# A gated attention and FFN kernel: two-tile attention steps, a later place for attention in the scheduler's order, weight splits finished by an accumulating DMA, and x operands kept in DRAM

## The chip, the cores and the metric

The kernel runs on one core of a Trainium2 chip. The metric is the device time of one execution in microseconds (us). Three executions of the kernel before are known; their median is 679.92 us.

## The reference, cut to what matters

```python
x = A_x                                            # 1 x 2048 x 512, float32
g = sigmoid((x * gate_w).sum(-1, keepdims=True))
qkv = x @ wqkv                                     # 512 x 1536; 32 heads of 16 channels
# query s looks at keys s, s-2, ..., s-14 (8 of them, dilation 2); masked where negative
a = softmax(q . k / 4) @ v  ->  2048 x 512  @ wo   # 512 x 512
b = (gelu_tanh(x @ w_gate) * (x @ w_up)) @ w_down  # 512 x 1792, 512 x 1792, 1792 x 512
out = g * a + (1 - g) * b
```

Everything is float32. The kernel splits each matmul operand into a high part, rounded to the matmul's float32r type, and a low part, the remainder, and multiplies high by high, high by low and low by high: three matmuls for each product.

## The kernel before, in words

**Parity halves.** Dilation 2 means that even and odd tokens never meet in attention. All work is done per parity (`par` 0 and 1), 1024 tokens each: 8 tiles of 128 tokens (`NP`), or 2 blocks of 512 (`blk`).

**Stages, in the order of the text.** (1) Six projections, `project(par, cb)`: `cb` 0 and 2 give q and k of one half of the heads, `cb` 1 gives v and the gate. Their results go to DRAM (`KS`, `QS`, `VS`). (2) `ffn(0)`: 14 steps `f` of `gate_up`, each with 7 products of 6 matmuls (a Strassen-like scheme over two weight matrices, gate and up: operands of x named a11, a12, a22, s1 to s4, operands of the weights named b11, b21, b22, t1 to t4), and from step 2 on four `down` pieces of 6 matmuls that belong to the pair of steps before. (3) `finish(0)`: 96 matmuls that add attention times `wo` onto the down result. (4) `ffn(1)` and `finish(1)`, the same for the odd tokens.

**Attention as filler.** `attention()` is a Python generator over 8 units (parity, 128 channels). For each unit it loads k, q and v in shifted slots, and does `scores` (per tile a product of 8 x 128 values and a reduction), `softmax`, and `mix` (per tile a product, three halving additions, and per four tiles a transpose whose result goes to DRAM, `OS`). All of that arithmetic is VectorE's. `pull(budget)` advances the generator after each projection tile, each group of products and each `down`; every `yield` gives the microseconds that a piece is reckoned at. So attention's instructions lie between FFN's. The framework's scheduler then simulates the program and takes ready instructions by their place in that order; every engine and every DMA queue executes its own list in order.

**Weights of a step.** `fetch(f)` loads gate and up weights (SP's DMA queue), `combine(f)` forms t1 to t4 with three VectorE subtractions, and `operands(par, f)` splits the seven operands one by one: ScalarE copies to the high part (line 68), GpSimd subtracts to the low part (line 69), and SP stores the pair to DRAM (`WS`, line 362). Parity 1 loads those pairs back (line 359) and neither combines nor splits again. `down_w` does the same for the down weights (`DS`, lines 368 and 374).

**VectorE's part of an FFN step.** `add` (line 390) reads a PSUM bank and thereby frees it, `hidden` multiplies (line 394) and, for parity 0, subtracts for the low part (line 397; for parity 1 GpSimd does that). There are four rotating PSUM banks (`p`) and four that accumulate (`acc0` to `acc3`).

**x operands.** `operands_0` forms s1 to s4 of parity 0 during the projections. `operands_1` forms all operands of parity 1 during the last FFN step and `finish(0)`: four loads, eight VectorE sums (lines 114 to 117), 14 ScalarE copies and 14 GpSimd subtractions.

Of the kernel before, what the change touches and what calls it, by code (L numbers as in the profile page):

```python
# [16 lines left out]
P = 128  # L17
# [12 lines left out]
WARM = 31  # L30
BT = 4
MASKED = -1e9 * DH ** 0.5

OPS = ("b11", "t1", "t2", "b21", "b22", "t3", "t4")
# [3 lines left out]
def tile_gated_mix(ctx: ExitStack, tc: tile.TileContext, xt, wqkv, wff, wo, out):  # L38
# [6 lines left out]
    BUFS = {"A": 16, "S": 16, "w": 14, "d": 4, "raw": 2, "t": 1, "hh": 6, "hl": 6, "c": 4, "s": 3,  # L45
            "r": 2, "rt": 4, "p": 4, "lg": 2}
    COLS = {"w": 2 * WQ, "c": 2 * WQ, "d": 1024, "t": 1024, "raw": WT}

    def tl(tag, dt=F32):
        return pool.tile([P, COLS.get(tag, 512)], dt, name=tag, bufs=BUFS[tag])  # L50

# [20 lines left out]
    KS, VS, QS, OS, WS, DS = {}, {}, {}, {}, {}, {}  # L72
    for par in range(2):
        for hh in range(2):
            for n, t in (("k", KS), ("v", VS)):
                t[par, hh] = dram.tile([2, W + S // 2, UC], F32, name=f"{n}s{par}{hh}")
                for c in range(2):
                    nc.gpsimd.dma_start(t[par, hh][c, :W], zero)
            QS[par, hh] = dram.tile([2, S // 2, UC], F32, name=f"qs{par}{hh}")
        for u in range(NU):  # L80
            for half in range(2):
                OS[par, u, half] = dram.tile([32, 4, BT * P], F32, name=f"os{par}{u}{half}")


    early = iter(["c", "rt"] * 99)
    X, WC = {}, {}

    def load_xk(kc, blk, first=False):
        hi, lo = tl("A", F32R), tl("A", F32R)
        X[0, blk, kc] = hi, lo  # L90
        for a, n in ((0, P), (P, 512 - P)) if first else ((0, 512),):
            raw = tl(next(early))
# [4 lines left out]
    def load_cb(cb, kc, eng, tag=None):  # L97
        hi, lo = tl("w", F32R), tl("w", F32R)
        WC[cb, kc] = hi, lo
        raw = tl(tag or "c")  # L100
        if cb == 1:
            n = 2 * WQ
            for hh in range(2):
                nc.sync.dma_start(raw[:, hh * WQ:(hh + 1) * WQ], wqkv[hh, 2, :, kc * WQ:(kc + 1) * WQ])
        else:
            n = 512
            nc.sync.dma_start(raw[:, :n], wqkv[cb // 2, kc // 2, :, kc % 2 * 512:kc % 2 * 512 + 512])
        return lambda: split(eng, hi[:, :n], lo[:, :n], raw[:, :n])

    def sums(par, kc, a, b, eng, put, eng2=None):  # L110

        t = tl("t")
        s1, s2, s3, s4 = t[:, :512], t[:, 512:], b[:, :512], a[:, 512:1024]
        eng.tensor_tensor(s1, b[:, :512], b[:, 512:1024], op=OP.add)
        eng.tensor_tensor(s2, s1, a[:, :512], op=OP.subtract)
        eng.tensor_tensor(s3, a[:, :512], b[:, :512], op=OP.subtract)
        eng.tensor_tensor(s4, a[:, 512:1024], s2, op=OP.subtract)
        for n, s in (("s1", s1), ("s2", s2), ("s4", s4), ("s3", s3)):
            hi, lo = tl("S", F32R), tl("S", F32R)
            split(eng2 or eng, hi, lo, s)  # L120
            put(n, hi, lo)
            yield

    def raw_pair(par, kc):
        ab = []
        for blk in range(2):
            raw = tl("raw")
            nc.sync.dma_start(raw[:, :1024].rearrange("p (a c) -> p a c", a=2), xt[2 * par + blk, :, kc:kc + 3:2, :])
            ab.append(raw)
        return ab  # L130

    XOP, nxt = {}, {}

    def load_x1():
        for kc in range(2):
            a, b = raw_pair(1, kc)
            for blk, raw in ((0, a), (1, b)):
                for i in range(2):
                    if blk == 1 and (kc, i) != (1, 1):
                        d = tl("d", F32R)  # L140
                        hi, lo = d[:, :512], d[:, 512:]
                    else:
                        hi, lo = tl("hh", F32R), tl("hl", F32R)
                    X[1, blk, kc + 2 * i] = hi, lo
                    split(nc.vector, hi, lo, raw[:, i * 512:(i + 1) * 512])

    def operands_0():
        for kc in range(2):
            a, b = raw_pair(0, kc)
            for _ in sums(0, kc, a, b, nc.vector, lambda n, hi, lo: XOP.__setitem__((n, kc), (hi, lo))):  # L150
                pass
# [3 lines left out]
    def operands_1(first):  # L155
        for kc in range(2):
            a, b = raw_pair(1, kc) if kc else first
            for n, raw in (("a11", a[:, :512]), ("a12", a[:, 512:1024]), ("a22", b[:, 512:1024])):
                nxt[n, kc] = tl("A", F32R), tl("A", F32R)
                split(nc.gpsimd, *nxt[n, kc], raw)  # L160
                yield
            yield from sums(1, kc, a, b, nc.vector, lambda n, hi, lo: nxt.__setitem__((n, kc), (hi, lo)), nc.gpsimd)
# [69 lines left out]

    def scores(par, u):
        k, q = LG[par, u]
        lg = pool.tile([P, NP, W, UH], F32, name="lg", bufs=2)
        for jj in range(NP):
            prod = pool.tile([P, W, UC], F32, name="prod")
            nc.vector.tensor_tensor(prod, k[:, jj:jj + W, :], q[:, jj, None, :].to_broadcast([P, W, UC]), op=OP.mult)  # L238
            nc.vector.tensor_reduce(lg[:, jj].rearrange("p w h -> p (w h)"),  # L239
                                    prod.rearrange("p w (h d) -> p (w h) d", d=DH), axis=AX.X, op=OP.add)  # L240
            yield 2.5
# [21 lines left out]
    def mix(par, u):  # L263
# [4 lines left out]
        tb = pool.tile([P, NP, UC], F32, name="tb")  # L268
        for jj in range(NP):
            if jj % BT == 0:  # L270
                o = pool.tile([P, BT, UC], F32, name="o")
            prod = pool.tile([P, W, UC], F32, name="prod")
            nc.vector.tensor_tensor(prod.rearrange("p w (h d) -> p w h d", d=DH),  # L273
                                    v[:, jj:jj + W, :].rearrange("p w (h d) -> p w h d", d=DH),
                                    lg[:, jj, :, :, None].to_broadcast([P, W, UH, DH]), op=OP.mult)
            yield 1.2
            nc.vector.tensor_tensor(prod[:, :4], prod[:, :4], prod[:, 4:], op=OP.add)  # L277
            nc.vector.tensor_tensor(prod[:, :2], prod[:, :2], prod[:, 2:4], op=OP.add)  # L278
            nc.vector.tensor_tensor(o[:, jj % BT], prod[:, 0], prod[:, 1], op=OP.add)  # L279
            yield 1.4  # L280

            if jj % BT == BT - 1:
                nc.vector.transpose(tb[:, jj + 1 - BT:jj + 1].rearrange("p t c -> p (t c)"),
                                    o.rearrange("p t c -> p (t c)"))
                for a in range(4):
                    nc.sync.dma_start(OS[par, u, jj // BT][:, a], tb[32 * a:32 * a + 32, jj + 1 - BT:jj + 1])
# [29 lines left out]
    def pull(budget, key=None):  # L316
        credit[0] += budget
        while credit[0] > 0 and (key is None or key not in done):
            c = next(fill, None)
# [11 lines left out]
    RAW = {}  # L331

    def fetch(f):
        raw = tl("raw")
        nc.sync.dma_start(raw[:, :1024], wff[f, :, :1024])
        RAW[f] = [raw]

    def combine(f):

        raw, t = RAW[f][0], tl("t")  # L340
        quart = raw[:, :1024].rearrange("p (a b) -> p a b", a=4)
        b11, b21, b12, b22 = (raw[:, i * 256:(i + 1) * 256] for i in range(4))
        t1, t3, t2, t4 = (t[:, i * 256:(i + 1) * 256] for i in range(4))
        sub = lambda o, a, b: nc.vector.tensor_tensor(o, a, b, op=OP.subtract)  # L344
        sub(t[:, :512].rearrange("p (a b) -> p a b", a=2), quart[:, 2:], quart[:, 0::2])
        sub(t2, b22, t1)
        sub(t4, b21, t2)
        RAW[f] = dict(b11=b11, b21=b21, b22=b22, t1=t1, t2=t2, t3=t3, t4=t4)
# [307 lines left out]
```

## Time and profile before

| | us |
|---|---|
| three runs | 678.1, 679.92, 680.22 (median 679.92) |
| the profiled execution, its own time | 680.39 |
| its span in the profile | 678.6 |
| PE, DVE, ACT, POOL busy in the span | 631.2, 584.4, 313.8, 236.1 |
| mean granted TensorE clock | 0.967 |

PE is TensorE's matmuls, PEld its weight loads, DVE is VectorE, ACT ScalarE, POOL GpSimd, SPq the DMA queue that SyncE issues. "idle before" is the time in which an engine stood still just ahead of the instructions of a group, and the arrow names what ended most of it. L390 is line 390 of the kernel before. Three stages can be told by the PE's lines: projections from 4.2 to 144.0 us, `ffn(0)` with `finish(0)` to 435.4 us, `ffn(1)` with `finish(1)` to 674.5 us.

### The profile page before, as it was taken

Reading aid. Unit: us, or ns where it says so; the run is one execution under the profiler, and the core shown is the slowest. Engines: PE = TensorE matmul, PEld = TensorE weight load, DVE = VectorE, ACT = ScalarE, POOL = GpSimd, SP = SyncE. Lnnn points to the kernel's source line nnn. Section 1 sums busy time; section 2 is a strip of 40 time slices with the busy share of each in tenths; the row PEclk is TensorE's granted clock in tenths of the full one; section 3 lists DMA queues with packets and bytes.
Section 4 is the critical chain, followed back from the end, with each engine's and each line's share of the span. In section 5 each row is a group of like instructions: output and inputs, shape, how many; then the busy total and the mean of one; then the engine's idle time right before and its main releaser. Section 6 shows DMA issues by size and latency. Waiting matters only on the chain.

```text
span 678.6 us, 8894 instructions
## 1 busy us (share of the span) xinstructions
PE 631.2 (93%) x2839; PEld 512.9 (76%) x2839; DVE 584.4 (86%) x714; ACT 313.8 (46%) x601; POOL 236.1 (35%) x198
## 2 busy tenths in 40 slices
PE   8998999996799979997989849999999999999997
PEld 6888998874587758875868637888777888887785
DVE  5439899879999999989999988998999999989432
ACT  4424442245446455655454564234434644454562
POOL 5204014066737364634471760023122221224220
PEclk9999999998799989998998978999999999999999
DMA  8885755597966665675457587776566766544163
GB/s 254 269 253 172 247 156 187 172 300 250 310 235 218 243 229 171 234 252 208 156 191 224 159 225 158 249 234 218 179 187 197 214 196 197 185 124 127 36 104 124
DMA packets 116046, 136.46 MB, mean 201 GB/s; under 512 B 42400, under 2 KB 68640, under 8 KB 116000
## 3 DMA queue, kind: packets, MB, share of 16 engines
q1 hardware_dynamic: 115488, 135.84, 63.8%
q8 instruction: 22, 0.36, 0.2%
q14 instruction: 24, 0.20, 0.1%
q0 software_dynamic: 512, 0.07, 0.1%
HBM read 81.80 MB, written 54.07 MB: 200 GB/s over the span
## 4 chain that ended last, share of the span: by engine, by line
DVE 41%; PE 38%; DMA 7%; issue 6%; ACT 4%; SPq 1%; POOL 1%; DVEq 0%; POOLq 0%; ACTq 0%
PE p L381 21%; DVE prod L273 6%; PE p L420 6%; PE acc L420 5%; DVE prod L238 5%; DVE prod L277 4%; DVE lg L239 4%; DMA raw<-xt 4%; PE acc L557 3%; PE p L557 3%; DVE t L344 3%; DVE c L394 3%; DVE c L390 2%; DVE prod L278 2%; DVE o L279 2%
## 5 line engine op out<-in xcount | busy, mean ns | idle before, releaser
L381 PE MATMUL p<-S,w 128*128 128x512 f32 x672 | 176.6, 406 | 10.2 <-DVE c L390 4.1
L381 PEld LDWEIGHTS p<-S,w 128*128 128x128 f32 x672 | 130.8, 195 | 42.8 <-DVE c L390 4.5
L381 PE MATMUL p<-A,w 128*128 128x512 f32 x504 | 135.6, 407 | 16.2 <-DVE c L390 16.0
L381 PEld LDWEIGHTS p<-A,w 128*128 128x128 f32 x504 | 97.1, 194 | 42.4 <-DVE c L390 20.0
L397 POOL TENSOR_TENSOR hl<-c,hh 128x512 fp32r<-128x512 f32 x28 | 44.7, 1595 | 168.5 <-ACT hh L396 141.4
L238 DVE TENSOR_TENSOR prod<-k,q 128x1024 f32<-128x1024 f32 x64 | 86.8, 1356 | 11.5 <-DMA q<-qs 10.6
L273 DVE TENSOR_TENSOR prod<-v,lg 128x1024 f32<-128x1024 f32 x64 | 81.5, 1273 | 6.7 <-DMA v<-vs 5.3
L420 PE MATMUL p<-d,hh 128*128 128x512 f32 x224 | 71.7, 405 | 10.5 <-ACT p L414 10.4
L239 DVE TENSOR_REDUCE lg<-prod 128x64 f32<-128x1024 f32 x64 | 77.7, 1214 | 1.1
L69 POOL TENSOR_TENSOR w<-t,w 128x256 fp32r<-128x256 f32 x56 | 58.4, 1056 | 48.2 <-ACT w L68 38.5
L396 ACT ACTIVATE hh<-c 128x512 fp32r<-128x512 f32 x56 | 35.3, 631 | 80.3 <-DVE c L394 80.0
L69 POOL TENSOR_TENSOR w<-raw,w 128x256 fp32r<-128x256 f32 x42 | 43.0, 1034 | 63.8 <-ACT w L68 60.6
L277 DVE TENSOR_TENSOR prod<-prod 128x512 f32<-128x512 f32 x64 | 59.0, 922 | 1.3
L420 PEld LDWEIGHTS p<-d,hh 128*128 128x128 f32 x224 | 43.0, 194 | 22.0 <-ACT p L414 11.8
L420 PE MATMUL acc<-d,hh 128*128 128x512 f32 x224 | 57.7, 394 | 0.7 <-ACT hh L396 0.7
L420 PEld LDWEIGHTS acc<-d,hh 128*128 128x128 f32 x224 | 41.8, 188 | 11.7 <-ACT hh L396 2.4
L394 DVE TENSOR_TENSOR c<-c 128x512 f32<-128x512 f32 x56 | 44.6, 796 | 5.2 <-ACT c L482 4.8
L385 ACT ACTIVATE s<-p 128x512 f32<-128x512 f32 x56 | 32.8, 593 | 26.2 <-PE p L381 26.2
L390 DVE TENSOR_TENSOR c<-p,s 128x512 f32<-128x512 f32 x56 | 38.0, 681 | 8.0 <-PE p L381 7.8
L420 PE MATMUL p<-d,hl 128*128 128x512 f32 x112 | 42.9, 394 | 0.0
L429 ACT ACTIVATE rt<-p 128x512 f32<-128x512 f32 x48 | 28.6, 595 | 29.4 <-PE p L420 28.0
L177 PE MATMUL p<-w,A 128*128 128x512 f32 (+2 forms) x192 | 38.5, 345 | 2.9 <-ACT w L68 1.1
(125 smaller groups left out, 1002.0 us busy)
## 6 DMA issues: line engine op xcount, KB each, us to landing
ws<-w SPq DMA_DIRECT2D x98, 256.0 KB, 2.9
w<-ws SPq DMA_DIRECT2D x98, 256.0 KB, 2.7
raw<-wff SPq DMA_DIRECT2D x14, 512.0 KB, 5.0
ds<-d SPq DMA_DIRECT2D x14, 512.0 KB, 3.9
d<-ds SPq DMA_DIRECT2D x14, 512.0 KB, 4.5
raw<-xt SPq DMA_DIRECT2D x12, 512.0 KB, 5.4
k<-ks SPq DMA_DIRECT2D x8, 512.0 KB, 5.0
q<-qs SPq DMA_DIRECT2D x8, 512.0 KB, 6.3
```

Of the source, the lines that this page charges most:

```text
L69: eng.tensor_tensor(lo, raw, hi.bitcast(F32), op=OP.subtract)
L177: nc.tensor.matmul(ps[:, :cn], a[:, t], w[:, c0:c0 + cn], start=(kc == 0 and n == 0), stop=(kc == KC - 1 and n == 2))
L238: nc.vector.tensor_tensor(prod, k[:, jj:jj + W, :], q[:, jj, None, :].to_broadcast([P, W, UC]), op=OP.mult)
L239: nc.vector.tensor_reduce(lg[:, jj].rearrange("p w h -> p (w h)"), prod.rearrange("p w (h d) -> p (w h) d", d=DH), axis=AX.X, op=OP.add)
L273: nc.vector.tensor_tensor(prod.rearrange("p w (h d) -> p w h d", d=DH), v[:, jj:jj + W, :].rearrange("p w (h d) -> p w h d", d=DH), lg[:, ...
L277: nc.vector.tensor_tensor(prod[:, :4], prod[:, :4], prod[:, 4:], op=OP.add)
L381: nc.tensor.matmul(ps, w_, a_, start=(start and kc == 0 and n == 0), stop=(kc == 1 and n == 2), skip_group_check=True)
L390: nc.vector.tensor_tensor(c, ps, s, op=OP.add)
L394: nc.vector.tensor_tensor(ge, ge, up, op=OP.mult)
L397: eng.tensor_tensor(hl_, ge, hh_.bitcast(F32), op=OP.subtract)
L420: nc.tensor.matmul(pp, a[:, ts], w, start=(i == 0 and n == 0 and gr == 0), stop=(i == 1 and n == 2), skip_group_check=True)
L557: nc.tensor.matmul(pa, a, b, start=False, stop=(u == NU - 1 and n == 2), skip_group_check=True)
```

## The change

1. *Two tiles per attention instruction.* `scores` and `mix` handle two token tiles in each VectorE instruction (`spans` gives overlapping windows of k or v), so half as many instructions do twice the elements each. `OS` is laid out so that `channels` reads it back with one DMA of 2 KB rows instead of four with rows of 128 bytes.
2. *Order.* `pull` runs the generator under a priority 150 places later (`BEHIND`).
3. *Weight splits.* `operands(f)` works on two groups (three and four operands side by side): ScalarE writes minus the high part into the low part's place, a GpSimd-issued DMA with `accum_op=add` adds the raw weights onto it, and ScalarE writes the high part. GpSimd's subtractions and the stores to and loads from `WS` and `DS` are gone; for parity 1 weights are fetched, combined and split anew.
4. *Queues.* Weight fetches, the reloads of x operands, and the output stores of parity 0 are issued by GpSimd.
5. *x operands of parity 1* are formed in `load_x1` at the start, stored to DRAM (`keep`) and reloaded one by one (`operands_1(n)`) in the last step of `ffn(0)`.
6. Buffers are laid out anew for that; the first loads find 12 places instead of 8.

The core of the diff:

```diff
+BEHIND = 150
+GROUPS = (("t1", "t2", "b11"), ("b22", "t3", "t4", "b21"))
...
+    def keep(n, kc, hi, lo):
+        x = XS[n, kc] = dram.tile([P, 1024], F32, name=f"x{n}{kc}")
+        nc.gpsimd.dma_start(x[:, :512], hi.bitcast(F32))
+        nc.gpsimd.dma_start(x[:, 512:], lo.bitcast(F32))
...
     def load_x1():
...
+            for n, x in sums(a, b):
+                hi, lo = pair("S")
+                split(nc.vector, hi, lo, x)
+                keep(n, kc, hi, lo)
...
+    def operands_1(n):
+        for kc in range(2):
+            t = tl("A" if n[0] == "a" else "S", F32R)
+            nc.gpsimd.dma_start(t.bitcast(F32), XS[n, kc])
+            XOP[n, kc] = t[:, :512], t[:, 512:]
...
+    def spans(t, jj):
+        a = t[:, jj:jj + W, :]
+        return bass.AP(a.tensor, a.offset, [a.ap[0], [UC, 2], [UC, W], [1, UC]])
...
     def scores(par, u):
-        for jj in range(NP):
-            prod = pool.tile([P, W, UC], F32, name="prod")
-            nc.vector.tensor_tensor(prod, k[:, jj:jj + W, :], q[:, jj, None, :].to_broadcast([P, W, UC]), op=OP.mult)
...
-            yield 2.5
+        for jj in range(0, NP, 2):
+            prod = pool.tile([P, 2, W, UC], F32, name="prod")
+            nc.vector.tensor_tensor(prod, spans(k, jj), q[:, jj:jj + 2, None, :].to_broadcast([P, 2, W, UC]), op=OP.mult)
+            yield 2.3
...
+            yield 2.3
...
     def pull(budget, key=None):
...
-            c = next(fill, None)
+            with tc.high_priority(offset=-BEHIND):
+                c = next(fill, None)
...
     def fetch(f):
-        nc.sync.dma_start(raw[:, :1024], wff[f, :, :1024])
+        nc.gpsimd.dma_start(r[:, 2::5], q[:, :2])
+        nc.gpsimd.dma_start(r[:, 3:5], q[:, 2:])
...
-    def operands(par, f):
+    def operands(f):
+        for i, ops in enumerate(GROUPS):
+            n = len(ops) * QW
+            w = tl(f"g{i}", F32R)
+            hi, lo = w[:, :n], w[:, n:2 * n]
...
+            nc.scalar.activation(lo, raw, AF.Copy, scale=-1.0)
+            nc.gpsimd.dma_start(lo.bitcast(F32), raw, accum_op=OP.add)
             yield
+            nc.scalar.activation(hi, raw, AF.Copy)
+            yield
...
-    def down_w(par, f):
+    def down_w(f):
         d = WD[f] = tl("d", F32R)
...
+        split(nc.gpsimd, d[:, :512], d[:, 512:], RD.pop(f))
...
+        def anew(*names):
+            if not par and f == FC - 1:
+                for n in names:
+                    operands_1(n)
...
+    def ahead():
+        combine(0)
+        AGAIN[0] = operands(0)
...
     def channels(par, u, half):
-        for b in range(4):
-            nc.sync.dma_start(o[32 * b:32 * b + 32].rearrange("p (m j) -> p m j", j=32), src[b])
+        nc.sync.dma_start(o, OS[par, u, half].rearrange("b i a c -> (b i) (a c)"))
...
-                    nc.sync.dma_start(out_v[2 * jj + par, :, c], r[:, c])
+                    (nc.sync if par else nc.gpsimd).dma_start(out_v[2 * jj + par, :, c], r[:, c])
```

## The prediction

> **What bounds the kernel now.** I first read the page's busy times (PE 93%, DVE 86%), then cut the span at the PE's lines into projections, parity 0 (`ffn(0)`, `finish(0)`) and parity 1. Busy time per stage (matmuls counted in brackets), with granted clock at the end:
>
> ```profile
> 4.20:144.00 139.80, 136.85 (x771) 118.63 (x770) 106.52 (x138) 52.31 (x125) 28.84 (x29) 1.00 0.72 223
> 144.00:435.40 291.40, 253.55 (x1022) 200.32 (x1021) 276.65 (x330) 151.44 (x296) 150.34 (x127) 0.92 0.67 218
> 435.40:674.50 239.10, 237.60 (x1021) 190.73 (x1019) 199.70 (x244) 108.16 (x180) 53.91 (x35) 1.00 0.56 169
> ```
>
> The columns are length, PE, PEld, DVE, ACT, POOL, clock, DMA. The parities have the same matmuls, but parity 0 takes 291.4 us and parity 1 239.1: 52.3 us are lost in parity 0, where DVE is 95% busy and the clock is 0.92. A clock of 0.92 over 291 us is worth 23 us; the rest is standing still. Parity 1 shows that the PE can be kept busy at full clock beside a DVE at 84%. Next, the waits (total us, times, longest):
>
> ```profile
> PEld p L381 <- DVE c L390: 24.5, 10, 5.2
> ...
> PE p L381 <- DVE c L390: 20.1, 7, 4.8
> ...
> PE p L420 <- ACT p L414: 10.4, 2, 7.7
> ```
>
> The PE waits for DVE's `add`, which frees a PSUM bank. The timeline shows one such wait:
>
> ```profile
> 313.47 1.49 DVE L344 TENSOR_TENSOR t<-raw,t 128x256 f32<-128x256 f32 x1
> 314.89 1.34 DVE L279 TENSOR_TENSOR o<-prod 128x128 f32<-128x128 f32 x1
> 316.15 0.41 DVE L344 TENSOR_TENSOR t<-raw,t 128x256 f32<-128x256 f32 x1
> 316.49 1.21 DVE L273 TENSOR_TENSOR prod<-v,lg 128x1024 f32<-128x1024 f32 x1
> 317.62 1.27 DVE L390 TENSOR_TENSOR c<-p,s 128x512 f32<-128x512 f32 x2
> ```
>
> The PE starts again at 318.95, 4.79 us late. DVE was behind with work that the PE does not need, and two of those instructions took over a microsecond more than their like. The twin at 316.15 took 0.41, not 1.49, and POOL was subtracting beside the slow ones. Sizes without that disturbance come from the groups in 420 to 440 us, where POOL has no work, and with it from those in 140 to 400:
>
> ```profile
> L273 DVE TENSOR_TENSOR prod<-v,lg 128x1024 f32<-128x1024 f32 x5 | 6.1, 1213 | 0.1
> L277 DVE TENSOR_TENSOR prod<-prod 128x512 f32<-128x512 f32 x5 | 3.4, 688 | 0.1
> L278 DVE TENSOR_TENSOR prod<-prod 128x256 f32<-128x256 f32 x5 | 2.1, 421 | 0.1
> L279 DVE TENSOR_TENSOR o<-prod 128x128 f32<-128x128 f32 x5 | 1.4, 288 | 0.1
> ```
>
> ```profile
> L397 DVE TENSOR_TENSOR hl<-c,hh 128x512 fp32r<-128x512 f32 x27 | 26.4, 977 | 3.4 <-ACT hh L396 3.3
> ...
> L277 DVE TENSOR_TENSOR prod<-prod 128x512 f32<-128x512 f32 x24 | 24.1, 1004 | 0.4
> ```
>
> So a DVE instruction costs about 0.16 us plus 1.03 ns per element (0.688 less 0.421 for 256 elements more), and beside POOL 0.3 us more on average.
>
> **Part by part: DVE in parity 0 (276.7 us now).** *Disturbance:* over the groups of 140 to 400 us, busy time less count times clean mean is 4.4 (L238), 3.1 (L273), 7.6 (L277), 4.5 (L278), 4.2 (L279), 7.8 (L397), 6.2 (L394) and 8.1 (L344): 46 us, over POOL's 127 instructions there, or 0.36 us each. The change leaves some 21 of those (14 down splits, 4 of `wo`, 3 masks): 8 us. Minus 38. *Two tiles:* three units of attention are 144 instructions here, 72 fewer at 0.16: minus 11.5. *Sums of `operands_1`* (L114 to L117, 15.5 us for 16, of which the early eight are clean): minus 10. *More attention:* a unit is reckoned at 45.4 before and 41.4 after, so the same budgets pull a tenth more, about 0.3 unit of 43 us: plus 13. Sum 230 us.
>
> **DVE in parity 1 (199.7 now).** Minus 11.5 for two tiles, minus 13 for the attention done earlier, plus 14 `combine` of 0.688 + 2 x 0.421 = 1.53, or 21, plus 5 for 14 more POOL subtractions: 201 us.
>
> **From DVE's load to time.** Per 237.6 us of matmuls DVE had 1.16 in parity 0, which then took 291.4 us, and 0.84 in parity 1, which took 239.1: 161 us for each unit between. At 230 us (0.97) the straight line gives 260 us. But most of the 52 us is sheer excess over the PE's time, so below 1 the loss should fall faster than the line; with none, it is 239. I take 254, nearer the line, since attention's instructions are now up to 2.3 us long and an `add` can stand behind one. Parity 1 (0.85) gives 241, and I add 1 for ACT's longer list.
>
> [...]
>
> **The order.** Of two ready instructions FFN's goes first. That costs nothing if attention is ready for `finish(0)`: by the budgets (108 in projections, 125 up to the last `down`) some five units are pulled by then and four are needed, so a delay of 150 places, about one step of 16 us, hides in a spare unit of 43. Without that cover, `finish(0)` would wait out those 16 us.
>
> **Weight splits.** Per step, seven ScalarE copies of 0.411 become four of 768 or 1024 elements:
>
> ```profile
> L396 ACT ACTIVATE hh<-c 128x512 fp32r<-128x512 f32 x56 | 35.3, 631 | 80.3 <-DVE c L394 80.0
> ...
> L68 ACT ACTIVATE w<-t 128x256 fp32r<-128x256 f32 x56 | 22.2, 411 | 10.8 <-DVE t L344 9.5 <-POOL w L69 1.3
> ...
> L78 POOL DMA_DIRECT2D ks<-zero x8 | 4.3, 540 | 1.1 <-DVE zero L62 0.9 <-issue 0.2
> ```
>
> At 0.22 per 256 elements they take 0.85 and 1.07, 3.8 us a step: ACT gains 0.95 a step in parity 0 (151 to 165 us of 254) and 4.5 with the down weights in parity 1 (108 to 171 of 242, or 70%). That lies beside PE's work while the copies that PE waits for pass in time. POOL loses 95 us of weight subtractions in parity 0.
>
> The accumulating DMA is not in this trace. Below, it is a copy:
>
> ```profile
> ws<-w SPq DMA_DIRECT2D x98, 256.0 KB, 2.9
> ...
> ds<-d SPq DMA_DIRECT2D x14, 512.0 KB, 3.9
> ```
>
> Above, it also reads its target, so twice 3.9. I take 5 us for 384 or 512 KB. It is issued early in step f for step f+1; about 13 us of cover remain, so either end costs nothing; past the cover each us costs 28 over the 28 steps. DMA volume falls by 66 MB (`ws`, `w`, `ds`, `d`) and grows by 11 (second weight fetch), 15 (x operands) and the 26 that the accumulation writes. SP's queue, which stood 99.5 us for POOL at L362 ahead of attention's loads, is freed of all that.
>
> POOL now issues five DMAs a step: two `fetch`, two accumulations, one `fetch_d`. The only row is 0.54 us, for 8 partitions. If the cost does not grow with partitions it stays there; if it grows in proportion, 128 cost 8.6. SP's issues of 128-partition loads stand at 0.39 to 0.55 in the timeline, so I take 1.1, near the low end. Queued behind such a DMA on POOL are the down split, the mask, and in parity 1 the low parts of `hidden`, for which `down` waits a step later. On DVE, `combine` waits for such a fetch, with `add` and attention queued behind it. Today that costs 1.3 us in all (L344 <- raw, the groups' idle column), and the fetch is issued half a step ahead as before, so I count nothing; 1 us late in each step would cost up to 28.
>
> **x operands, start.** Eight more VectorE splits and 28 DMAs of 256 KB. None of it stands ahead of the first projections; DMA engines are at 0.86 in the first 40 us, and 4.2 MB at 250 GB/s may push the first k and q loads back by up to 17 us, where DVE is nearly idle (5.4 of 20 us between 20 and 40). PE's cost: 0, up to 5 if the loads for `cb` 1 are late. The reloads, 7.3 MB (some 36 us at 200 GB/s), are hidden by the last step and `finish(0)`; uncovered, they cost a few us at one place.
>
> **Sum.** 4.2 (head) + 140 + 254 + 242 + 4.1 (tail) = 644 of span, and 1.8 around it as now (680.39 less 678.6): 646. The profiled execution stands 0.5 above the median, which changes nothing. Ends: 239 for both parities gives 628; parity 0 on the straight line, parity 1 at 250 and 3 us more at the start give 663.
>
> **Rivals.** *ACT takes DVE's place.* PE's next product needs W's copy and the bank seeds (L414 already holds it for 10.4 us), and longer instructions stand in that list. For it: ACT at 70% in parity 1. Against: PE has other groups of 6 matmuls between. If each step loses 1 us, 28 steps give 674; the same comes out if the accumulation outlasts its cover by 1 us.
>
> *POOL becomes the bound, and the kernel is slower.* In parity 1 POOL has per step two subtractions of 1.6 (L397), a down split of 1.6 and five issues of x: 4.8 + 5x against 16 us. It decides from x = 2.3 on; x = 2.7 uses up nearly the whole gain, and x = 3 costs 14 x 3.8 = 53 us in parity 1 and some in parity 0, so about 700. For it: x is between 0.54 and 8.6. Against: SP's issues. [...]
>
> *The change does not do what it says.* If readiness and not place decides DVE's order, the `add` waits stay where both are ready: that is the straight line, 652, within the forecast's own range.
>
> **Chances.** Forecast 0.60 (628 to 663); ACT or the accumulation late 0.17 (664 to 677); no change 0.03; slower 0.20, mostly POOL. About 0.3% (2 us) is what a measurement of this kernel can tell from no change. Range 626 to 690: it leaves out the dearer half of the slow cases and a little below.
>
> **What would show it.** DVE under 235 us in parity 0, L390's `add` no longer PE's longest wait, clock near 1.00, parity 0 near 254 us and parity 1 near 242; DMA issues on POOL near 1 us. Wrong if POOL is over 90% busy in parity 1, if `hi`/`lo` tiles or their DMA end PE's waits, or if parity 0 stays over 275 us.

## The result and the profile after

The changed kernel takes 688.15 us (median of four runs, 684.21 to 689.42), the kernel before beside it 679.27: ratio 1.0122 [1.0076, 1.0168]. It is slower by 1.2%; the forecast was 646. Of all timed runs below one, of e6, was a slow one (696.56 us at the lowest clock of its four), and e6's median leaves it out. The profiled execution has a span of 687.2 us against 678.6. Cut at PE's lines as before, with PE's standstill between the parities left out (the windows view of the kernel after; columns are length, PE, PEld, DVE, ACT, POOL, clock, DMA share, GB/s):

```profile
4.20:150.20 146.00, 139.49 (x772) 120.32 (x771) 113.86 (x120) 58.21 (x129) 45.14 (x58) 0.99 0.86 264
150.20:415.40 265.20, 245.61 (x1021) 193.06 (x1019) 241.38 (x254) 156.78 (x248) 99.04 (x109) 0.98 0.64 173
424.50:683.40 258.90, 246.70 (x1020) 196.59 (x1020) 184.21 (x188) 150.77 (x241) 122.18 (x112) 0.96 0.49 122
```

So the difference of 8.6 us of span is made of plus 6.2 in the projections (139.8 before), minus 26.2 in parity 0 (291.4), plus 9.1 in a standstill that was not there, and plus 19.8 in parity 1 (239.1); the tail gives 0.3 back. Of the gain of 37 us forecast for parity 0, 26 came. It was spent in three places for which the sum had almost nothing. In parity 1 VectorE has 15 us less work than before, and the stage is 20 us longer. PE's column shows how: the same matmuls take 246.7 us there instead of 237.6, at a clock of 0.96 instead of 1.00, so 9.1 of the 19.8 us are slow matmuls behind pauses, and 10.7 are pauses.

Who waits for whom (the waits of the kernel after: total us, times, longest):

```profile
DVE raw L404 <- DMA raw<-wff: 24.8, 12, 5.4
...
PEld p L435 <- DVE c L444: 21.6, 11, 3.7
ACT d L76 <- DMA r<-wff: 21.1, 6, 7.9
...
PE p L435 <- DVE c L444: 17.0, 9, 3.2
...
DVE raw L151 <- DMA raw<-xt: 12.5, 2, 12.3
...
PE p L435 <- ACT s L662: 9.0, 1, 9.0
```

PE and PEld wait for the same banks, so each pause shows in both lines. The `add` (L444, L390 before) is still the largest item of PE's own waits, 17.0 us in 9 waits where it was 20.1 in 7. Three waits for transfers are new or have grown: `combine` for weights (1.3 us before), the down split (L76) for its weights (2.4 before), and `sums` (L151) for x. The last line is the standstill between the parities. Its timeline:

```profile
410.48 5.48 POOL L77 TENSOR_TENSOR d<-r,d 128x512 fp32r<-128x512 f32 x1 [1.44 <-ACT d L76]
...
416.26 0.55 POOL L398 DMA_DIRECT2D r<-wff  x1 [0.30 <-POOL d L77]
...
418.62 0.90 POOL L398 DMA_DIRECT2D r<-wff  x1
421.45 0.63 ACT L76 ACTIVATE d<-r 128x512 fp32r<-128x512 f32 x1 [7.86 <-DMA r<-wff]
...
423.88 1.06 ACT L662 ACTIVATE s<-p 128x512 f32<-128x512 f32 x2
...
424.51 2.07 PE L435 MATMUL p<-A,g 128*128 128x512 f32 x4 [8.96 <-ACT s L662]
```

A GpSimd subtraction took 5.48 us; one of the same shape at 277.49 us, with no VectorE instruction beside it, took 1.26. The down-weight fetch (L398) is behind it on GpSimd's list, ScalarE's copy of those weights waits 7.86 us for the fetch, and behind that copy on ScalarE's list stand the output copies (L662) that free PE's banks. The subtraction explains some 4 of the 9 us (5.48 less 1.26, an estimate). The rest is the fetch itself, which takes 5.2 us from its issue at 416.26 to the copy at 421.45 (the median of these fetches is 3.1), and two more copies of weights on ScalarE ahead of L662.

### The profile page after: what moved, and what is told of

The parts are those of the page before. It is cut to its first block, busy times and chain, and to the rows that moved or that the text cites. A ratio compares the mean times of both kernels' runs of the same rounds, so it can differ in the third digit from the quotient of the medians.

```text
span 687.2 us, 8278 instructions
## 1 busy us (share of the span) xinstructions
PE 635.1 (92%) x2839; PEld 513.2 (75%) x2839; DVE 546.4 (80%) x572; ACT 370.7 (54%) x623; POOL 275.5 (40%) x294
## 4 chain that ended last, share of the span: by engine, by line
PE 37%; DVE 21%; DMA 18%; issue 11%; ACT 6%; POOL 4%; SPq 2%; DVEq 0%; POOLq 0%; ACTq 0%
PE p L435 22%; PE acc L474 6%; PE p L474 6%; DMA raw<-wff 5%; DVE prod L325 4%; DVE raw L404 3%; DMA g<-raw 2%; DVE prod L329 2%; DMA raw<-xt 2%; DMA raw<-wqkv 2%; PE acc L651 2%; DMA v<-vs 2%; PE p L651 2%; DVE c L448 1%; DVE prod L331 1%
## 5 line engine op out<-in xcount | busy, mean ns | idle before, releaser
L435 PE MATMUL p<-S,g 128*128 128x512 f32 x672 | 176.3, 406 | 15.0 <-ACT p L510 5.8
L435 PEld LDWEIGHTS p<-S,g 128*128 128x128 f32 x672 | 129.8, 195 | 48.9 <-ACT p L510 7.9
L435 PE MATMUL p<-A,g 128*128 128x512 f32 x504 | 135.9, 409 | 20.8 <-DVE c L444 11.8
L435 PEld LDWEIGHTS p<-A,g 128*128 128x128 f32 x504 | 98.1, 197 | 47.6 <-DVE c L444 15.1
L421 POOL DMA_DIRECT2D g<-raw x56 | 50.3, 898 | 157.4 <-ACT g L420 141.7
L325 DVE TENSOR_TENSOR prod<-v,lg 128x2048 f32<-128x2048 f32 x32 | 74.2, 2318 | 6.1 <-DMA v<-vs 5.6
L404 DVE TENSOR_TENSOR raw<-raw 128x256 f32<-128x256 f32 (+1 forms) x84 | 56.7, 677 | 24.9 <-DMA raw<-wff 24.8
L289 DVE TENSOR_TENSOR prod<-k,q 128x2048 f32<-128x2048 f32 x32 | 74.4, 2324 | 1.2 <-DMA qs<-r 1.0
L291 DVE TENSOR_REDUCE lg<-prod 128x128 f32<-128x2048 f32 x32 | 72.9, 2279 | 0.1
L77 POOL TENSOR_TENSOR d<-r,d 128x512 fp32r<-128x512 f32 x28 | 51.3, 1838 | 33.3 <-ACT d L76 32.5
L420 ACT ACTIVATE g<-raw 128x1024 fp32r<-128x1024 f32 (+1 forms) x56 | 53.2, 950 | 13.1 <-DVE raw L404 10.5
L444 DVE TENSOR_TENSOR c<-p,s 128x512 f32<-128x512 f32 x56 | 37.6, 681 | 25.6 <-PE p L435 25.6
L423 ACT ACTIVATE g<-raw 128x1024 fp32r<-128x1024 f32 (+1 forms) x56 | 53.0, 946 | 0.0
L474 PEld LDWEIGHTS acc<-d,hh 128*128 128x128 f32 x224 | 41.9, 188 | 10.7 <-ACT hh L450 1.1
```

Of the source, the lines that this page charges most:

```text
L77: eng.tensor_tensor(lo, raw, hi.bitcast(F32), op=OP.subtract)
L289: nc.vector.tensor_tensor(prod, spans(k, jj), q[:, jj:jj + 2, None, :].to_broadcast([P, 2, W, UC]), op=OP.mult)
L291: nc.vector.tensor_reduce(lg[:, jj:jj + 2].rearrange("p j w h -> p (j w h)"), prod.rearrange("p j w (h d) -> p (j w h) d", d=DH), axis=AX. ...
L325: nc.vector.tensor_tensor(prod.rearrange("p j w (h d) -> p j w h d", d=DH), spans(v, jj).rearrange("p j w (h d) -> p j w h d", d=DH), lg[: ...
L420: nc.scalar.activation(lo, raw, AF.Copy, scale=-1.0)
L421: nc.gpsimd.dma_start(lo.bitcast(F32), raw, accum_op=OP.add)
```

## The experiments

Medians of timed runs; PE's stages from each profile. The standstill is that between the parities. The diffs are abridged: `/` joins values of several lines, and words in brackets stand for the rest of an edit.

| kernel | us | ratio to before | projections | parity 0 | standstill | parity 1 |
|---|---|---|---|---|---|---|
| before | 679.27 | | 139.8 | 291.4 | 0 | 239.1 |
| after | 688.15 | 1.0076 to 1.0168 | 146.0 | 265.2 | 9.1 | 258.9 |
| e1 | 712.45 | 1.0455 to 1.0528 | 147.1 | 282.9 | 2.6 | 271.0 |
| e2 | 686.47 | 1.0087 to 1.0157 | 146.0 | 263.6 | 8.5 | 257.9 |
| e3 | 673.19 | 0.9905 to 0.9953 | 139.4 | 270.9 | 0 | 257.0 |
| e4 | 687.42 | 1.0080 to 1.0181 | 152.3 | 259.4 | 8.7 | 258.9 |
| e5 | 687.70 | 1.0101 to 1.0222 | 145.7 | 264.4 | 9.1 | 256.4 |
| e6 | 688.62 | 1.0120 to 1.0179 | 146.2 | 271.4 | 0.9 | 259.7 |
| e7 | 747.62 | 1.0986 to 1.1112 | 147.2 | 292.3 | 2.6 | 292.8 |
| e8 | 666.32 | 0.9807 to 0.9883 | 139.0 | 261.5 | 0 | 255.5 |
| e9 | 677.34 | 0.9979 to 1.0010 | 139.1 | 259.6 | 0 | 271.2 |
| e10 | 657.07 | 0.9678 to 0.9711 | 138.3 | 261.9 | 0 | 246.0 |
| e11 | 677.04 | 0.9970 to 1.0010 | 139.2 | 281.7 | 0 | 246.0 |
| e12 | 678.42 | 0.9981 to 1.0022 | 138.8 | 263.1 | 0 | 266.7 |
| e13 | 653.86 | 0.9599 to 0.9665 | 139.2 | 261.9 | 0.5 | 244.6 |
| e14 | 653.98 | 0.9598 to 0.9670 | 137.8 | 256.8 | 0.3 | 248.2 |
| e15 | 661.71 | 0.9719 to 0.9792 | 139.4 | 265.9 | 0 | 250.2 |
| e16 | 663.02 | 0.9729 to 0.9803 | 139.0 | 260.6 | 0 | 253.7 |

**Four first questions: the queue, the pace, the stores, the order.**

e1:
```diff
 fetch:   -nc.gpsimd.dma_start(r[:, 2::5], q[:, :2])   +nc.sync.dma_start(...)   (both halves)
 fetch_d: -nc.gpsimd.dma_start(RD[f], ...)             +nc.sync.dma_start(...)
```


> The changed kernel with the weight fetches (gate and up, and down) issued by SP again instead of GpSimd; nothing else. Theory A (late fetches: GpSimd's list holds them back, combine waits on VectorE and the add behind it keeps a PSUM bank): VectorE's wait of 24.8 us for raw falls under 6, the 9 us stall at the start of parity 1 falls under 2, and the time falls from 688 to 668 (663 to 675). Theory B (VectorE overfull in parity 1 because attention's pieces are pulled too early): within 3 us of 688. Theory C (28 stores at the start fill the DMA engines): within 2 us of 688.

24 us slower than after. The standstill shrank from 9.1 to 2.6, but `combine`'s wait grew from 24.8 to 49.7 us, the longest from 5.4 to 12.0, since the weight fetch now stands on SyncE's list with everything that list carries. Here GpSimd is the better queue for the weights.

e2:
```diff
-yield 2.3 / 1.2 / 1.1
+yield 2.9 / 1.5 / 1.4      (scores and mix)
```


> The changed kernel with attention reckoned dearer: its yields are 2.9, 1.5 and 1.4 instead of 2.3, 1.2 and 1.1, so a unit counts 51 instead of 41 and is pulled a quarter more slowly. Theory B: the last mix ends near 645 us instead of 599, the four stalls between 480 and 600 us (9 us, and 7 us of half clock) go, and the time falls to 677 (672 to 681), unless finish(0) now waits for attention. Theory A: within 3 us of 688. Theory C: within 2 us of 688.

1.7 us less than after, inside both intervals. It could not be otherwise: in the trace PE, VectorE, ScalarE and GpSimd each execute the same instructions in the same order as in the kernel after, VectorE all 572 of them. These budgets, a quarter dearer, do not move attention; that the scheduler takes it up as soon as its data and buffers are there is the likely reason.

e3:
```diff
 def keep(n, kc, hi, lo):
+    if XS:
+        XS[n, kc] = next(iter(XS.values()))
+        return
```


> The changed kernel with one of the 14 x operands of parity 1 stored to DRAM instead of all (2 stores instead of 28); all reloads read that one, so parity 1 computes with the wrong operands; the amount of arithmetic and of reloads is the same. Theory C: projections take 140 us as before the change instead of 146, and the time falls to 682 (680 to 684). Theories A and B: the first stage is not theirs; if the stores cost nothing, 688 within 2 us.

This kernel leaves out 26 of the 28 stores, and all reloads read the one operand that is stored. The projections are back at 139.4 us, the standstill is gone, and the kernel is 15 us faster than after. The stores cost more than the 6 us that show where they are.

e4:
```diff
-BEHIND = 150
+BEHIND = 0
```


> The changed kernel with BEHIND = 0, so attention keeps its place in the order. If the later place helps as the prediction had it (the add goes ahead of attention): 8 to 15 us slower, about 699, and the wait of PE for add (17 us) grows above 25. If it is the place that hurts (attention late, then everything at once): faster, about 680. If VectorE's order is decided by what is ready: within 3 us of 688.

0.7 us from after, so nothing in the total. The units' `mix` ends behind the same `add`s as in the kernel after (0, 2, 12, 20, 28, 34, 41 and 48 of 56). But the order is not without effect: 144 of VectorE's 572 places hold another instruction, the projections are 6.3 us longer (PE waits 7.8 us for ScalarE's copies for the gate, where it waits 0.7 in the kernel after) and parity 0 is 5.8 us shorter. The later place helps one stage by as much as it costs the next.

**What the waits for weights are worth.**

e5:
```diff
 ffn.more:  +combine(f + 1)   ahead of operands(f + 1)
            -combine(f + 2)   behind them
```


> The kernel after, with combine(f) moved from the end of step f-2 to the start of step f-1, just before operands(f), so that the weight fetch has half a step (about 8 us) more. Theory A (the fetch arrives late, combine waits for it on VectorE with the add that frees PE's bank queued behind): combine's wait for raw<-wff falls from 24.8 us to under 8, PE's and PEld's waits for the add from 38.6 us together to under 25, total 676 to 682. Rival B (the add is late because long attention instructions stand ahead of it): combine's wait falls, PE's waits for the add stay over 33 us, total within 2 us of 687. Third way: operands(f) now start later and the adding DMA loses its cover, PE waits for g tiles, total over 692.

687.7, no change, with 36.5 us of waits for the `add` (PE and PEld added, as in the expectation: 38.6 in the kernel after). That looks like rival B, but `combine`'s wait fell only from 24.8 to 22.8: the edit hardly gave the fetch more time. What that wait costs is not told by this run.

e6:
```diff
 fetch_d:      -nc.gpsimd.dma_start(RD[f], ...)   +nc.sync.dma_start(...)
 finish:       -(nc.sync if par else nc.gpsimd)   +nc.sync
```


> The kernel after, with the down-weight fetch and parity 0's output stores issued by SyncE again; weight fetches and adding DMAs stay on GpSimd. Theory A (the standstill between the parities comes from small transfers queued behind GpSimd's work): the gap of 9.1 us falls under 3 and the second one of 3.3 us to under 1, the rest stays, total 675 to 679. Rival B (something else is late there, the reload of x or the first weights): the gap stays over 6 us, total within 2 us of 687.

The standstill fell from 9.1 to 0.9 us, but that does not show its cause, and the total did not fall. Parity 1 starts at 422.7 us, only 1.8 earlier than in the kernel after; the rest is that parity 0 ends 6.4 us later, since a pause of 2.9 us at 160 us has become one of 8.6. There too ScalarE's copy of down weights stands ahead of copies that PE waits for, and it waits 7.0 us for its fetch, now on SyncE's list. The slow subtraction is still there, with 5.27 us, 10.5 us ahead of the end of parity 0.

What speaks for the chain is a comparison of all traces. In the four with a standstill of over 8 us (after, e2, e4, e5) one subtraction of 5.5 to 5.6 us begins 5 to 6 us ahead of the end of parity 0. In e3, e8, e10 and e12 to e16, with 0.5 us or none, no down split within 10 us of that end takes over 3.9 us. e9 is the exception: it has a subtraction of 5.79 us there and no standstill, but PE pauses 3.6 us some 4 us later.

e7:
```diff
-nc.scalar.activation(lo, raw, AF.Copy, scale=-1.0)
-nc.gpsimd.dma_start(lo.bitcast(F32), raw, accum_op=OP.add)
+nc.gpsimd.tensor_tensor(lo, raw, hi.bitcast(F32), op=OP.subtract)
```


> The kernel after, with the low parts of the weights by a GpSimd subtraction on 768 or 1024 elements instead of ScalarE's negative copy and the adding DMA. Theory A (the adding DMA is a gain, because GpSimd's subtractions stretch VectorE's instructions): VectorE's sum in parity 0 goes from 259 us to over 285, parity 0 from 265 to over 275, total 698 to 715. Rival B (the adding DMA's 5 us of landing hold the raw buffer and make everything after it late): the wait of GpSimd's raw<-wff issue for g<-raw (21.0 us) vanishes, combine waits under 8 us, total under 682.

Theory A, and dearer than expected: 59 us slower than after. In the groups of that kernel GpSimd's subtraction costs 144.5 us, and VectorE's load in parity 0 is 286.1 us instead of 241.4:

```profile
L422 POOL TENSOR_TENSOR g<-raw,g 128x1024 fp32r<-128x1024 f32 (+1 forms) x56 | 144.5, 2586 | 179.3 <-ACT g L420 140.0 <-DMA qs<-s 30.8 <-DVE c L447 7.2
```

By the profiles 27 us of it are in parity 0 and 34 in parity 1, while the standstill gives 6.5 back; in parity 1 the kernel before has no such subtraction. The adding DMA is the part of the change that pays.

**The stores, done but later.**

e8 (and from here on the base):
```diff
 def keep(n, kc, hi, lo, after=None):
+    if after is not None:                    # after = g[:1, 1, :8], for a11, a12, a22
+        for c in (slice(0, 8), slice(512, 520)):
+            nc.gpsimd.dma_start(x[:1, c], after)
(and keep_x1() is called behind project(1, 1), not behind project(0, 1))
```


> The kernel after, with 12 of the 28 stores of x operands (those of a11, a12, a22; 3 MB) held back until the gate of parity 1 is known, by a tiny write to the same place, so that they go out after about 110 us and not between 16 and 48. Theory A (DMA engines busy 0.97 between 20 and 60 us make the loads of the projections late): stage 1 falls from 145.9 to 141 to 143, total 682 to 685, and 673 to 677 if the gap between the parities goes with it as it did with 26 stores left out. Rival B (the 16 stores of s1 to s4 alone fill the DMA engines): stage 1 stays over 144.5, total within 2 us of 687.

666.3 us: 22 below after, 12 below before. The projections are at 139.0. In the kernel after these 12 stores are issued from 16.5 to 48.7 us, among the 16 of s1 to s4; their later place in the text did not hold them back:

```profile
16.54 1.13 POOL L169 DMA_DIRECT2D xa<-hh  x2 [4.54 <-ACT hh L76]
...
48.19 0.54 POOL L170 DMA_DIRECT2D xa<-hl  x1
```

In e8 they go out from 113.8 us on. What they did is seen in the windows 20:40 and 40:60 of the kernel after and then of e8:

```profile
20.00:40.00 20.00, 18.13 (x79) 14.41 (x78) 14.85 (x17) 7.11 (x13) 12.37 (x18) 1.00 0.97 335
40.00:60.00 20.00, 20.00 (x115) 17.48 (x114) 6.65 (x11) 6.49 (x12) 4.79 (x9) 1.00 0.97 304
```

```profile
20.00:40.00 20.00, 19.16 (x83) 15.23 (x82) 18.71 (x24) 9.79 (x18) 12.61 (x18) 1.00 0.87 277
40.00:60.00 20.00, 20.00 (x120) 17.72 (x119) 9.91 (x16) 9.02 (x18) 1.20 (x3) 1.00 1.01 320
```

VectorE's work in these 40 us goes from 21.5 to 28.6 us, although the DMA engines (last columns) are still nearly full. In the kernel after, VectorE stood still for x:

```profile
57.70 0.69 DVE L151 TENSOR_TENSOR raw<-raw 128x512 f32<-128x512 f32 x1 [12.32 <-DMA raw<-xt]
58.43 0.63 ACT L76 ACTIVATE S<-raw 128x512 fp32r<-128x512 f32 x1 [8.91 <-DVE raw L151]
```

`operands_0` came late, the next weights of the projections could be loaded only at 69.18 (56.50 in e8), since they need its raw buffer (SyncE waits for the split of s), and attention lost the time as well. In e8 the longest wait of `sums` for x is 3.8 us.

e16:
```diff
-keep("a11", kc, *X[1, 0, kc], g[:1, 1, :8])    (behind project(1, 1))
+keep("a11", kc, *X[1, 0, kc], g[:1, 0, :8])    (behind project(0, 1))
```


> Kernel e8 with the 12 stores held only until the gate of parity 0 is known (about 75 us instead of 106). Theory A (the stores hurt because they crowd the loads of 20 to 60 us; once these are through, their place does not matter): stage 1 139 to 140.5, total within 4 us of 666. Rival B (e8's 21 us came from an order that happened to fall well): stage 1 about 139, but the rest over 6 us longer, total over 672.

663.0 with an earlier place for the same stores and the call where it was: the gain is not one lucky order. In e3, e8 and e16 the standstill goes too, and with it the subtraction of 5.5 us (there at most 3.9); why it falls better there stays open.

**Parity 1.**

e9:
```diff
 gate_up:    +mark.append(...); nc.vector.tensor_copy(mark[-1], c12[:1, :1])
 load_kq, mix: +nc.vector.tensor_copy(t[:1, 0, :1], mark[-1])   ahead of load_slots
 scores, mix: -yield 2.3 / 1.2 / 1.1   +yield 2.5 / 1.3 / 1.2
```


> Kernel e8 with attention tied to FFN's progress: one VectorE copy of a single element per FFN step marks it, and the loads of k and v of a unit wait for the latest mark; budgets raised by 4 to 9%. By the instruction lists the last mix then ends behind the 54th of 56 adds (before: 54th, after: 48th, e8: 50th). Theory A (two-tile attention is taken as soon as its data are there, so it ends earlier and leaves VectorE as full as before while it lasts): spread out, PE's and PEld's waits for the add fall from 38.1 us in e8 to under 28, parity 1 from 255.5 us to under 250, total 655 to 662. Rival B (the waits come from long instructions ahead of the add, wherever they stand): total within 3 us of e8's 666, or over 669 when finish waits for a later unit.

My theory fell. The waits for the `add` did fall, from 38.1 to 27.0 us over the whole kernel, but parity 1 grew from 255.5 to 271.2: in its place PE waited for ScalarE's copies, GpSimd's low parts and once 3.6 us for an adding DMA, and its matmuls took 251.1 us instead of 242.3, at a clock of 0.96 instead of 0.99. Spreading attention is no remedy here.

e10:
```diff
-w = WG.pop(f)
+w = WG[0] if par else WG.pop(f)      (and no fetch, combine, operands in parity 1)
```


> Kernel e8, leaving out that parity 1 fetches, combines and splits its gate and up weights: all its 14 steps use the operands of the first. Theory A (forming the weights a second time is what parity 1 lost): ScalarE's sum there falls by some 50 us, VectorE's by 21, parity 1 falls from 255.5 to under 245, near the 239 of before, total under 657. Rival B (attention's long instructions and GpSimd's other subtractions do it): parity 1 stays over 250, total over 661.

This kernel leaves out the second forming, so parity 1 computes with the weights of one step. Parity 1 falls by 9.5 us, to 246.0, between the two expectations.

e15:
```diff
-for i, _ in enumerate(operands(f + 1)):
+for i, _ in enumerate(range(4) if par else operands(f + 1)):
```


> Kernel e8, leaving out only the split of parity 1's gate and up weights (ScalarE's copies and the adding DMAs; fetch and combine stay, and all steps use the operands of the first). It parts the 9.5 us of e10 in two. Theory A (ScalarE's copies of 0.85 to 1.05 us stand ahead of the copies and seeds that PE waits for): parity 1 falls from 255.5 to 246 to 249, total 657 to 660, ScalarE's sum there by 45 us or more. Rival B (combine on VectorE and its wait for the fetch do it): parity 1 stays over 252, total over 663.

250.2: by these profiles the split has 5.3 of the 9.5 us and fetch and `combine` 4.2. The profiled execution of e15 is 3.5 us above its median; by the medians (666.32, 661.71, 657.07) it is 4.6 and 4.6. About half each, then, and neither alone.

e11 (on the kernel before):
```diff
-for jj in range(NP):        prod [P, W, UC]
+for jj in range(0, NP, 2):  prod [P, 2, W, UC]     (scores and mix, as in the change)
```


> The kernel before with two tiles per attention instruction and nothing else of the change (the transposes go through a buffer of half the size). By the prediction's arithmetic: 72 VectorE instructions fewer in each parity at 0.16 us, 11.5 us, at 161 us per unit of load 7.8 us in parity 0, total 670 to 673. Theory A (attention then ends earlier, behind the 46th add and not the 54th, and VectorE stays as full while it lasts, with instructions of 2.3 us ahead of the add): total within 4 us of 679, or slower.

677.0, as theory A gave it, but as two effects: parity 0 is 9.7 us shorter (the prediction's arithmetic: 7.8) and parity 1 6.9 longer, with 35 us less VectorE work in it:

```profile
143.40:425.10 281.70, 249.98 (x1021) 195.40 (x1020) 272.26 (x247) 148.69 (x295) 169.78 (x126) 0.96 0.69 229
425.10:671.10 246.00, 239.52 (x1021) 191.85 (x1019) 164.30 (x160) 108.42 (x181) 51.16 (x35) 0.99 0.52 161
```

e12 (e8 with one tile):
```diff
-for jj in range(0, NP, 2):  prod [P, 2, W, UC]
+for jj in range(NP):        prod [P, W, UC]
```


> Kernel e8 with attention of one tile per instruction; all else of the change stays. By the prediction's arithmetic VectorE has 11.5 us more in each parity, some 8 us of it in parity 0's time: total 673 to 677. Theory A (instructions of 2.3 us, up to 3.4 beside GpSimd, stand ahead of the add): PE's and PEld's waits for the add fall from 38.1 to under 30 us although VectorE has more to do, total 660 to 667. If the last unit (behind the 56th add by the list) comes late for finish, a gap of 5 us or more shows there.

678.4, against theory A: waits for the `add` are 45.6 us, not fewer. The total is near the prediction's arithmetic (673 to 677), but by luck: that had some 8 us in parity 0, and measured are 1.6 there and 11.2 in parity 1. Here one tile per instruction makes parity 1 11.2 us longer, where in the kernel before it made it 6.9 shorter. So the cost that e11 shows in parity 1 is not a property of long instructions that could be carried from one kernel to the other.

**A version that beats both.**

e13:
```diff
 operands:  +x = WS[f, i] = dram.tile([P, 2 * n], F32, ...)
            +nc.sync.dma_start(x, w[:, :2 * n].bitcast(F32))
+operands_again(f):  nc.sync.dma_start(w[:, :2 * n].bitcast(F32), WS[f, i])    for parity 1 (no fetch, combine or split there)
```


> Kernel e8 with the split gate and up weights of parity 0 stored to DRAM (SyncE, 1.8 MB a step, 25.7 MB in all) and loaded again in parity 1 by SyncE, as the kernel before did, in place of a second fetch, combine and split. Theory A (of parity 1's 16 us over before, 9.5 are the second forming): parity 1 falls from 255.5 to 244 to 249, parity 0 stays within 5 us of 261.5, total 655 to 662. Rival B (the stores wait on SyncE's list for the adding DMA's landing, with attention's loads behind them, and the DMA engines have 51 MB more): parity 0 rises over 270 us, total over 668.

e14:
```diff
-nc.sync.dma_start(w[:, :2 * n].bitcast(F32), WS[f, i])
+nc.gpsimd.dma_start(w[:, :2 * n].bitcast(F32), WS[f, i])
```


> Kernel e13 with the loads of parity 1 issued by GpSimd (28 issues at 0.6 to 0.9 us, where the adding DMAs and fetches had 56). Theory A (SyncE's loads must wait for a free weight buffer and hold up attention's loads behind them): parity 1 is 2 us or more shorter than in e13. Rival B (nothing waits there): within 2 us of e13 in parity 1.

653.9 and 654.0 us: ratio 0.9632 [0.9599, 0.9665] to before, 34 us below the change as it was made. The windows of e13:

```profile
143.40:405.30 261.90, 245.29 (x1021) 194.42 (x1019) 232.30 (x244) 152.74 (x243) 87.42 (x103) 0.97 0.88 272
405.80:650.40 244.60, 239.64 (x1020) 190.65 (x1020) 176.25 (x163) 115.86 (x194) 85.60 (x68) 1.00 0.45 153
```

Against e8, parity 1 falls by 10.9 us at full clock. Parity 0 pays nothing, although the DMA share there is 0.88 instead of 0.66. The expected obstacle in e14's theory A was not there, and rival B did not hold either: with the loads on GpSimd parity 1 was 3.6 us longer and parity 0 5.1 shorter.

## Why the prediction was wrong, by its steps

**x operands at the start ("PE's cost: 0, up to 5"): wrong.** Taken 0, measured 6.2 in the projections, and e3 and e8 show 15 and 22 us over the whole kernel. I named the mechanism (4.2 MB between the loads of the first 40 us) and got its size and its cover wrong. 4.2 MB are the 16 stores of s1 to s4; the other 12, 3.1 MB, went out in the same 32 us, and holding those alone (e8) brought the 22 us. As cover I took VectorE's idle time; in the kernel after its longest stop is 12.3 us of waiting for x behind those stores, and the loads of the next weights needed the buffer that `operands_0` held.

**The standstill between the parities: missing.** "Queued behind such a DMA on POOL are the down split, the mask" looks one way only. That a DMA is also behind the down split, at 5.48 us instead of 1.3, and ScalarE's copies behind that DMA, I did not ask. The timeline and the comparison of traces show this chain; no run takes it away alone, and e6 does not.

**From DVE's load to time: failed in parity 1.** I had 201 us of load and 241 of time; measured were 184 and 258.9. Two points, one from each parity, made a line in which load was the only cause. Without a second forming of the weights (e10) and with the old store and reload (e13) the same matmuls take 246.0 and 244.6. So "I add 1 for ACT's longer list" is the term that was too small: the second forming cost 9.5 us, about half of it in the split. ScalarE's load was even below what I reckoned (151 against 171 us). A load of 58% still cost time; that its long copies stand in line with those that PE waits for is the likely way, and only e15's 5 us or so are shown. Of the remaining 10 us, 3.4 go with the early stores and the standstill (258.9 to 255.5 in e8). That e11's 6.9 and e10's 9.5 add up to e8's 16.4 over before may be chance, given e12; this remainder stays open.

**Parity 0: the line was right, I left it.** The load was 241.4 and not 230. The straight line gives 239.1 + 161 x (241.4 - 199.7) / 237.6 = 267.4; measured 265.2. It holds within 7 us in parity 0 of other kernels too (e7: 297.6 against 292.3, e11: 288.3 against 281.7, e13: 261.2 against 261.9). I took 254 at 230, below the line (260), on the thought that most of the loss is excess over PE's time. The rest of the miss is the load, and the term that was too small is "more attention": parity 0 has 24 score tiles and 29 to 30 mix tiles before, 32 and 30 to 32 after, so about 0.6 unit more and not 0.3. At the prediction's 43 us a unit these are 13 us more. It came from the budgets, and e2 shows that they do not place attention.

**Right:** the adding DMA. Taken 5 us, measured 5.1 for 512 KB and 4.5 for 384 KB; and GpSimd's subtractions do stretch VectorE's instructions (e7: 286.1 us of load instead of 241.4 in parity 0). DMA issue on GpSimd: taken 1.1 us, measured 0.52 to 0.90 (means of the groups, from `vs<-zero` to L421), so the rival in which GpSimd becomes the bound is out (122 us busy of 258.9). The issues (columns: busy us, mean ns; then GpSimd's idle time before):

```profile
L421 POOL DMA_DIRECT2D g<-raw x56 | 50.3, 898 | 157.4 <-ACT g L420 141.7
```

The order costs nothing: right for the total (e4), but it gains nothing either. Merging two tiles saves what the rows said: 2.28 us for 2048 elements where two of 1024 took 2.43, or 0.15 us for each pair where I took 0.16 (VectorE's row for 424 to 600 us in the kernel after):

```profile
L325 DVE TENSOR_TENSOR prod<-v,lg 128x2048 f32<-128x2048 f32 x12 | 27.4, 2280 | 0.2
```

**The rivals.** Late ScalarE was priced at 28 us and shows about 5 in one parity. Apart from that the loss came from none of the rivals: the slower case that I priced had GpSimd as the bound, and what happened was a slower start, one transfer caught behind a stretched subtraction, and new work in a stage that had been free.

## What to carry to other kernels

Parity 1 ran at its bound before (237.6 us of matmuls in 239.1), so it had nothing to gain. Before putting work into such a stage (here a second forming of weights, 9.5 us by e10), price each instruction by whose list it joins, not by the engine's load, and keep the store and reload if the DMA engines have room (e13: share 0.88 in parity 0, at no cost there). New stores belong behind the loads that start the pipeline, and an engine that is idle there may be waiting for those very loads (VectorE in the kernel after: 12.3 us). Undo the parts of a mixed change one by one: here stores made too early (22 us) and weights formed twice (10 us) hid the gain of the adding DMA.

## What was not expected of the hardware

In the kernel after, PE's clock was halved 3.3 us into the standstill from 415.4 to 424.5 us and stayed so for 4.6 us after it (windows):

```profile
414.00:416.00 2.00, 1.54 (x7) 0.93 (x5) 2.00 (x4) 0.00 (x0) 1.96 (x1) 1.00 0.44 109
...
418.00:420.00 2.00, 0.00 (x0) 0.00 (x0) 2.00 (x4) 0.00 (x0) 1.52 (x3) 0.71 0.98 367
420.00:422.00 2.00, 0.00 (x0) 0.00 (x0) 0.79 (x2) 0.55 (x2) 0.00 (x0) 0.50 1.09 219
...
426.00:428.00 2.00, 2.00 (x6) 1.61 (x5) 1.76 (x2) 0.47 (x1) 2.00 (x5) 0.50 0.99 131
428.00:430.00 2.00, 2.00 (x8) 1.54 (x7) 0.00 (x0) 1.97 (x4) 1.95 (x5) 0.73 1.01 404
```

From these shares the granted clock falls to 0.50 at 418.84, 3.3 us after PE stops, and is back at 1.00 at 429.08, 4.6 us after it starts, so the standstill of 9.1 us costs about 2.3 us more in slow matmuls. In the projections of the kernel after, half clock followed a much shorter gap, of 1.80 us at 92.1 us (window of 10 us):

```profile
90.00:100.00 10.00, 8.20 (x56) 7.99 (x55) 9.93 (x13) 5.15 (x13) 1.46 (x2) 0.83 1.04 302
```

0.83 over 10 us is 3.4 us at half clock. In e13's parity 1, where PE's longest wait is 1.2 us, the clock stays at 1.00. In the traces of before and after, half clock went with where a gap lay. In the kernel after the stretches at 0.50 that begin between the first and the last matmul begin at 94.57, 162.84, 244.76, 299.37, 418.84, 435.90, 534.89 and 589.50 us. They last 3.41 us each, but for the fifth with 10.24 and the sixth with 6.83, and from start to start it is 20, 24, 16, 35, 5, 29 and 16 times 3.413 us. The six of the kernel before, of 3.41 to 13.65 us, fit steps of the same length. In these two traces a step at full clock in which PE stood still for 1.8 us or more was followed by one at 0.50 in all 13 cases, a step with 1.63 us or less in none; of three with 1.65 to 1.69 us one was. The gap of 1.80 us lies within one step; a gap of 3.08 us at 277.4 us in the same kernel falls on two, 1.50 and 1.58 us, and the clock stayed at 1.00.

In the kernel after, whose two-tile products take VectorE 2.3 us, a GpSimd subtraction of 128x512 (the down splits of L77) took anything from 1.26 to 5.48 us (median 1.36 over 28); GpSimd's next instruction came 5.78 us after the start of the slow one, so the span is not an artefact of the record. I had priced only what GpSimd does to VectorE. The length of VectorE's instructions is what differs between the kernels: in the two with one tile per attention instruction (before and e12) the longest of GpSimd's 68 subtractions of 128x512 takes 2.38 and 2.32 us, in each of the 16 with two tiles 3.34 to 5.79. So by these traces merging the tiles, which saves VectorE 0.15 us a pair, also brought the slow subtraction.
